# The wide stage of a fused attention and expert kernel: a chunk's small products in one visit of TensorE

## The chip, the cores and the metric

One core of one Trainium2 chip runs the kernel. The metric is device time in microseconds (us); several runs give a median. The profile is one execution, and its engines are called PE (TensorE), PEld (TensorE's weight load), DVE (VectorE), ACT (ScalarE), POOL (GpSimd) and SP (SyncE).

## The reference, cut to what matters

Three layers run in a row over 4 x 768 tokens: a linear attention with a decaying state for each of 8 heads, a gated layer of width 1536, and a top-1 mixture of 8 experts.

```
for t in range(S):                       # attention, S = 768, D = 48
    cur = einsum('bhd,bhe->bhde', u * k_t, v_t)
    y_t = einsum('bhd,bhde->bhe', r_t, state + cur)
    state = w * state + einsum('bhd,bhe->bhde', k_t, v_t)
gate = sigmoid(x @ w_gate); val = x @ w_val
x = (gate * val) @ w_out
idx = argmax(normed(x) @ normed(emb).T / tau)
out[idx == e] = gate_w * (relu(x[idx == e] @ w1[e]) @ w2[e])
```

## The kernel before

The tokens go in 24 chunks of 128, six to a batch. The attention of a chunk is a chunked form: decay tables are multiplied into r and k, a product of k and r gives the chunk's scores, products of k and v (the **state products**) give what the chunk adds to the state, and y is made of a part from the state and a part from the masked scores. A chunk has two halves of 64 tokens. All these are small f32 products of 64x64 (48 wide for the states), and each lies in one quarter of PE's 128x128 array: its operands lie in one half of the partitions (the **row half**), its result in one half of the output's partitions (the column half). An f32 product of this kind leaves two MATMUL records in the trace, so 8 products read x16.

The functions around the change are these. `at_p` issues POOL's table products (lines 542 to 555). `at_P` makes the state products of a chunk (line 617), 16 of them, or 8 in the last chunk of a batch, where the second half's state isn't needed. `at_Y1` makes 8 products of the masked scores with v (line 637) for the two off-diagonal halves of y, and `at_Y2` makes up to 16 products with the states (line 637, read as `py<-ld,T`) and 8 more with the scores (line 637, `py<-Am,ld`). `native_A` makes the 16 score products of the next chunk (line 594). `at_T` adds the state products to the running state on DVE (lines 628 to 633). `at_X` splits y into two parts for the next layer (lines 686 to 692).

The gated layer is the large work. In the **wide stage** it takes 512 tokens at a time, in 12 steps of 128 features: nine `pgate` products of 128x512 (line 721), ACT's sigmoid (line 730), nine `pval` products, DVE's product (line 734), ACT's and DVE's split into two parts (lines 736 and 738), and then the output products `o` of the step before (line 766). A counter called tick goes up by one after `pgate` and once more after `pval`. A table made ahead sets at which tick a stage of which chunk is emitted: six ticks, three steps, to a chunk. Stage 4 (state products, Y1, then `at_T`) falls between `pgate` and `pval`, stage 5 (Y2, the next chunk's scores) between `pval` and `o`. The words "P visit" and "Y visit" stand below for these two. DVE's dot products for the routing (line 783) are spread over the ticks and stand behind whatever a tick has emitted before.

PSUM has these tiles: two buffers in turn for `pgate` and `pval` (pool `ps_gv`, tag `gv`), four for `o`, and one each of `a0` and `a1`, in which y takes columns 0 to 255 and the state products, then the scores, take columns 256 on. A new tile in a buffer waits until the readers of the old one are done. The constant EARLY is 9; stages of chunks 9 to 23 run in the wide stage.

Of the kernel before, what the change touches and what calls it, by code (L numbers as in the profile page):

```python
# [8 lines left out]
F32 = mybir.dt.float32  # L9
# [7 lines left out]
ALU = mybir.AluOpType  # L17
# [18 lines left out]
EARLY = 9  # L36
# [26 lines left out]
def kernel(  # L63
# [14 lines left out]
    nc = tc.nc  # L78
    P = 128
    NCH = att.shape[0]  # L80
    NT, DM = out.shape
    CPB = 6
# [33 lines left out]
    def follow(ins, before):  # L116

        tc.add_manual_dep(
            ins, before.name,
            mybir.DependencyInfo(mybir.DependencyClass.NoSync, mybir.DependencyReason.DATA), reason="order",  # L120
        )
# [181 lines left out]
    if True:  # L303
# [7 lines left out]
        halves = [slice(HALF * i, HALF * i + HALF) for i in range(2)]  # L311
# [32 lines left out]
        ps_gv = ph1.enter_context(tc.tile_pool(name="ps_gv", bufs=2, space=bass.MemoryType.PSUM))  # L344
        ps_o = ph1.enter_context(tc.tile_pool(name="ps_o", bufs=1, space=bass.MemoryType.PSUM))
        ps_a = ph1.enter_context(tc.tile_pool(name="ps_a", bufs=1, space=bass.MemoryType.PSUM))
# [8 lines left out]
        ld = {}  # L355
# [107 lines left out]
        for i in range(7):  # L463
            n = 1 << i
# [3 lines left out]
        tabKt = c1.tile([P, 8, 48], F32, name="tabKt")  # L468
# [54 lines left out]
        yps = {}  # L523
        pms = {}

        def fields(t):
            rT = t[:, 0:512].rearrange("p (a n) -> p a n", a=4)
            kT = t[:, 512:1024].rearrange("p (a n) -> p a n", a=4)
            kt = t[:, 1024:1408].rearrange("p (h d) -> p h d", h=8)
            v = t[:, 1408:1920].rearrange("p (h d) -> p h d", h=8)  # L530
            r = t[:, 1920:2304].rearrange("p (h d) -> p h d", h=8)
            return rT, kT, kt, v, r
# [9 lines left out]
        def at_products(c):  # L542
            rT, kT, kt, v, r = fields(ld[c])
            if c < EARLY:

                nc.gpsimd.tensor_tensor(r, r, kt, op=ALU.mult)
                nc.gpsimd.tensor_tensor(r, r, ubt, op=ALU.mult)
                rk = ld[c][:, 0:1024].rearrange("p (b a n) -> p b a n", b=2, a=4)
                nc.vector.tensor_tensor(rk, rk, tabs, op=ALU.mult)
            else:  # L550
                nc.gpsimd.tensor_tensor(rT, rT, tabR, op=ALU.mult)
                nc.gpsimd.tensor_tensor(kT, kT, tabK, op=ALU.mult)
                nc.gpsimd.tensor_tensor(r, r, kt, op=ALU.mult)
                nc.gpsimd.tensor_tensor(r, r, ubt, op=ALU.mult)
            nc.gpsimd.tensor_tensor(kt, kt, tabKt, op=ALU.mult)

        def at_s1(c):
            at_sd(c)
            at_diag(c)
# [23 lines left out]
        def native_A(c):  # L583

            rT, kT, kt, v, r = fields(ld[c])
            if c > PERM:
                pas = [t[:, 256:512] for t in yps[c - 1]]
            else:
                pool, tag = (ps_o, f"o{1 if c else 0}") if c < PERM else (ps_a, "a")
                pas = [pool.tile([P, 512], F32, tag=f"{tag}{h}", name=f"pa{h}") for h in range(2)]  # L590
            for p in range(4):
                for h in range(2):
                    for i in halves:
                        nc.tensor.matmul(  # L594
                            pas[h][i, p * HALF:p * HALF + HALF], kT[halves[h], p, i], rT[halves[h], p, i],
                            start=True, stop=True,
                        )
            return pas

        def native_mask(c, pas):  # L600
            Am = ams[c]
            for h in range(2):
# [3 lines left out]
                    pas[h][:, 0:4 * HALF].rearrange("p (a n) -> p a n", a=4),  # L606
                )

        def at_P(c):

            rT, kT, kt, v, r = fields(ld[c])
            yps[c] = [ps_a.tile([P, 512], F32, tag=f"a{h}", name=f"py{h}") for h in range(2)]
            pm = [yps[c][1 - i][:, 256:448].rearrange("p (a d) -> p a d", a=4) for i in range(2)]
            for p in range(4):
                for i in range(1 if c % CPB == CPB - 1 else 2):
                    for h in range(2):
                        nc.tensor.matmul(  # L617
                            pm[i][halves[h], p, :], ld[c][halves[i], 1024 + 48 * (2 * p + h):1088 + 48 * (2 * p + h)],
                            v[halves[i], 2 * p + h, 0:48], start=True, stop=True,
                        )  # L620
            pms[c] = pm

        def at_T(c):

            pm = pms.pop(c)
            t0, t1, t2 = (t[:, :, 0:48] for t in (states[c % 2], states[2], states[(c + 1) % 2]))
            if c % CPB == 0:
                nc.vector.tensor_copy(t1, pm[0])
            else:
                nc.vector.tensor_tensor(t1, t0, pm[0], op=ALU.add)  # L630
            if c % CPB < CPB - 1:
                nc.vector.tensor_tensor(t2, t1, pm[1], op=ALU.add)
                nc.vector.tensor_tensor(t2, t2, pw[:, 7, :].unsqueeze(2).to_broadcast([P, 4, 48]), op=ALU.mult)

        def y_part(c, p, h, i, w, x, begins, last):
            o = yps[c][h][halves[h ^ (p % 2)], p // 2 * P + HALF * i:p // 2 * P + HALF * i + HALF]
            q = nc.tensor.matmul(o, w, x, start=begins, stop=last, skip_group_check=True)  # L637
            return getattr(q, "ins", q)

        def chunk_part(c, p, h, i, begins, last):  # L640
            rT, kT, kt, v, r = fields(ld[c])
            n = 2 * p + h
            y_part(c, p, h, i, v[halves[i], n, :], ams[c][halves[i], n, :], begins, last)

        def at_Y1(c):
            for p in range(4):
                for h in range(2):
                    chunk_part(c, p, h, 1 - h, c % CPB == CPB - 1 and h == 0 and p < 2, not (c % CPB or h == 0))

        def at_Y2(c):  # L650
            rT, kT, kt, v, r = fields(ld[c])
            lead = None
            for i in range(2):
                if c % CPB or i:
                    for p in range(4):
                        for h in (1, 0):
                            d = slice(HALF * h, HALF * h + 48)
                            q = y_part(
                                c, p, h, i, (states[2] if i else states[c % 2])[d, p, :], rT[d, p, halves[i]],
                                False, i != h,  # L660
                            )
                            lead = lead or q
                            if h == 0:
                                follow(q, lead)
            for p in range(4):
                for h in (1, 0):
                    chunk_part(c, p, h, h, False, c >= PERM or (h == 1 and p >= 2))
            if c < PERM:
                py = yps[c]
                y3 = early[:, 3 + c % 2, :]  # L670
                nc.scalar.activation(y3, py[1][:, P:2 * P], AF.Copy)
                for k in range(3):
                    nc.tensor.matmul(
                        py[k // 2][:, k % 2 * P:k % 2 * P + P], early[:, k, :], y3,
                        start=False, stop=True, skip_group_check=True,
                    )
# [33 lines left out]
        open_y = []  # L710
        scores = {}
# [310 lines left out]
        def AFTER(c):  # L1022
            return 3 if c < EARLY else 2
# [41 lines left out]
        begins = {}  # L1065
# [16 lines left out]
        def at_stage(c, st):  # L1082
            if st == -2:
                at_p(c)
            elif st == 1:
                at_s1(c)
            elif st == 2:
                native_mask(c, scores.pop(c) if c in scores else native_A(c))
                open_y.clear()
            elif st == 4:  # L1090
                at_P(c)
                at_Y1(c)
                at_T(c)
                open_y.append(c)
            elif st == 5:
                at_Y2(c)
                if c < NCH - 1:
                    scores[c + 1] = native_A(c + 1)
                else:
                    open_y.clear()  # L1100
            elif st == 6:
                at_X(c)
                if c % 2 == 1:
                    at_D(c)
                if c == 7:
                    list(warm_up(WARM_WIDE))
                if c != EARLY - 1 and c + AFTER(c) < NCH:
                    load_chunk(c + AFTER(c))
# [37 lines left out]
        while threads:  # L1146
            th = min((t for t in threads if met(t[3])), key=lambda t: t[0])
            now, t0, dt, need, name, gen = th
# [67 lines left out]
        for f in range(XF):  # L1216
# [16 lines left out]
            elif f == 5:  # L1233
                q = nc.vector.tensor_scalar(lim[:, 0, :], wd, W_MIN, None, op0=ALU.is_ge)
# [28 lines left out]
        for c in CAPS:  # L1263
            n = 3 if c <= 3 * P else 4
# [152 lines left out]
        for f in range(XF):  # L1417
# [4 lines left out]
            if f == 1:  # L1422
                q = nc.sync.dma_start(out=x0, in_=xs[FIRST:CAP])
# [166 lines left out]
```

## Time and profile before

| | |
|---|---|
| time, median of 3 runs | 813.88 us (813.58 to 814.77) |
| the profiled execution's own time | 814.92 us |
| its span, first to last instruction | 813.0 us |
| PE busy | 794.2 us, 98% of the span |
| PEld busy | 703.7 us, 87% |
| DVE busy | 508.8 us, 63% |
| ACT busy | 318.2 us, 39% |
| POOL busy | 226.8 us, 28% |

The profiled execution took 814.92 us, of which 1.9 us lie outside its span. A busy PE is one with a record in flight; since records of matmuls overlap, what PE work costs is read from the distance between starts, not from the length of a record.

### The profile page before, as it was taken

What the parts mean: (1) busy time and instruction counts of PE and PEld (TensorE: products, weight loads), DVE (VectorE), ACT (ScalarE), POOL (GpSimd) and SP (SyncE); (2) the same over time, 40 slices, a digit from 0 to 9 for tenths busy, and PEclk for the clock granted to TensorE, in tenths of its full rate; (3) what the DMA queues carried; (4) which work ended last, traced back from release to release, by engine and by line L of the source; (5) the groups of instructions that cost most, each with busy time, mean ns of one, the idle gap of its engine ahead of it and who ended that gap; (6) DMA issues with size and microseconds to landing.
All of it is one profiled execution on the core that took longest, in us unless ns stands there. A gap on an engine that the chain in (4) does not pass through costs nothing.

```text
span 813.0 us, 17075 instructions
## 1 busy us (share of the span) xinstructions
PE 794.2 (98%) x6864; PEld 703.7 (87%) x6864; DVE 508.8 (63%) x1248; ACT 318.2 (39%) x659; POOL 226.8 (28%) x257
## 2 busy tenths in 40 slices
PE   7899999999999999999999999999999999999997
PEld 6789998888888888888888888889889989899996
DVE  6999965666556665577576548745585555556640
ACT  5788643221231213212322224234374454566541
POOL 5622137244251515244443210200320210201202
PEclk8699999999999999999999999999999999999999
DMA  8749733122222122030402002270556556465401
GB/s 330 285 175 366 265 129 140 60 70 79 69 79 70 60 75 94 14 115 26 143 2 70 21 31 79 98 239 20 167 153 238 167 193 222 146 204 173 145 1 56
DMA packets 36575, 103.02 MB, mean 127 GB/s; under 512 B 4406, under 2 KB 19462, under 8 KB 33417
## 3 DMA queue, kind: packets, MB, share of 16 engines
q1 hardware_dynamic: 32871, 91.92, 33.1%
q0 software_dynamic: 3616, 9.93, 3.3%
q8 instruction: 56, 0.92, 0.5%
q14 instruction: 30, 0.25, 0.1%
q10 hardware_dynamic: 2, 0.00, 0.0%
HBM read 84.09 MB, written 16.28 MB: 123 GB/s over the span
## 4 chain that ended last, share of the span: by engine, by line
PE 77%; issue 12%; DVE 5%; ACT 3%; POOL 2%; DMA 1%; POOLq 0%; SPq 0%; ACTq 0%; DVEq 0%
PE o L766 18%; PE pval L721 16%; PE pgate L721 16%; PE ph L971 7%; PE y L1344 7%; PE py L637 3%; PE pgv L721 3%; PE py L617 2%; POOL out_dram L1377 2%; DVE x L430 1%; PE py L594 1%; PE y L1358 1%; PE warm L376 1%; DVE x L429 1%; DMA ldr<-in_att_dram 1%
## 5 line engine op out<-in xcount | busy, mean ns | idle before, releaser
L721 PE MATMUL pval<-xt,gv 128*128 128x512 f32 x540 | 137.6, 399 | 0.0
L721 PE MATMUL pgate<-xt,gv 128*128 128x512 f32 x540 | 136.3, 397 | 0.0
L766 PE MATMUL o<-wo,gth 128*128 128x384 f32 x480 | 125.9, 343 | 0.0
L721 PEld LDWEIGHTS pval<-xt,gv 128*128 128x128 f32 x540 | 100.4, 188 | 24.4
L721 PEld LDWEIGHTS pgate<-xt,gv 128*128 128x128 f32 x540 | 100.7, 188 | 19.3
L971 PE MATMUL ph<-xk,we 128*128 128x384 f32 (+6 forms) x576 | 116.7, 349 | 0.0
L783 DVE SCALAR_TENSOR_TENSOR prod<-xr,embb 128x384 f32<-128x384 f32 x168 | 104.6, 623 | 4.2 <-DMA embb<-embd 1.1
L971 PEld LDWEIGHTS ph<-xk,we 128*128 128x128 f32 x576 | 101.9, 188 | 5.9 <-issue 1.2
L1344 PE MATMUL y<-we,ht 128*128 128x384 f32 (+1 forms) x528 | 101.4, 339 | 0.0
L736 ACT ACTIVATE gth<-sgw 128x512 fp32r<-128x512 f32 x60 | 37.9, 631 | 146.0 <-DVE sgw L734 146.0
L1344 PEld LDWEIGHTS y<-we,ht 128*128 128x128 f32 (+1 forms) x528 | 91.7, 187 | 1.0
L766 PEld LDWEIGHTS o<-wo,gth 128*128 128x128 f32 x480 | 86.1, 188 | 4.2
L730 ACT ACTIVATE sgw<-pgate 128x512 f32<-128x512 f32 x60 | 35.8, 597 | 126.5 <-PE pgate L721 121.6
L734 DVE TENSOR_TENSOR sgw<-pval,sgw 128x512 f32<-128x512 f32 x60 | 41.4, 690 | 65.6 <-PE pval L721 54.0
L766 PE MATMUL o<-wo,gtl 128*128 128x384 f32 x240 | 81.1, 338 | 0.0
L575 POOL TENSOR_TENSOR Am<-near,sd 128x512 f32<-128x512 f32 (+4 forms) x24 | 27.2, 1132 | 165.1 <-DVE sd L563 122.1
L1377 POOL DMA_INDIRECT out_dram<-yo,xrow x26 | 26.6, 1022 | 166.5 <-ACT yo L1374 154.4
L885 DVE TENSOR_TENSOR we<-wraw,we 128x768 fp32r<-128x768 f32 x64 | 61.7, 967 | 13.6 <-ACT we L882 12.7
L976 DVE SCALAR_TENSOR_TENSOR ht<-ph,ht 128x384 fp32r<-128x384 f32 (+1 forms) x56 | 31.8, 568 | 61.2 <-ACT ht L975 61.0
L738 DVE TENSOR_TENSOR gtl<-sgw,gth 128x512 fp32r<-128x512 f32 x60 | 45.2, 754 | 29.5 <-ACT gth L736 29.4
L975 ACT ACTIVATE ht<-ph 128x384 fp32r<-128x384 f32 (+1 forms) x56 | 28.1, 503 | 81.8 <-PE ph L971 80.4
L721 PE MATMUL pgv<-xt,gv 128*128 128x256 f32 x432 | 58.2, 288 | 0.4 <-DVE gv L438 0.2
(251 smaller groups left out, 1130.5 us busy)
## 6 DMA issues: line engine op xcount, KB each, us to landing
wraw<-in_wex_dram SPq DMA_DIRECT2D x64, 384.0 KB, 3.3
ld<-in_att_dram SPq DMA_DIRECT2D x20, 1152.0 KB, 5.8
raw<-in_wgv_dram SPq DMA_DIRECT2D x12, 768.0 KB, 8.1
w2f<-in_wex_dram SPq DMA_DIRECT2D x10, 768.0 KB, 6.6
xs<-zt SPq DMA_DIRECT2D x8, 750.0 KB, 7.4
raw<-in_wout_dram SPq DMA_DIRECT2D x6, 768.0 KB, 11.4
xrow<-xs SPq DMA_DIRECT2D x6, 600.0 KB, 5.2
ldr<-in_att_dram SPq DMA_DIRECT2D x3, 1152.0 KB, 6.4
```

What stands on the lines that cost most here:

```text
L721: nc.tensor.matmul(pg, a, x[:, k, b, :], start=(n == 0), stop=(n == 8))
L730: nc.scalar.activation(sg, p0, AF.Sigmoid)
L734: nc.vector.tensor_tensor(sg, p1, sg, op=ALU.mult)
L736: nc.scalar.activation(hi, sg, AF.Copy)
L738: q = nc.vector.tensor_tensor(lo, sg, hi, op=ALU.subtract)
L766: nc.tensor.matmul(po[g][t], gt[a][:, ts_], w[:, f % 2, b, :], start=(f == 0 and n == 0), stop=(f == NF - 1 and n == 2))
L783: nc.vector.scalar_tensor_tensor(prod, xr[:, t, 0:DM], 1.0, embb[0][:, e], op0=ALU.mult, op1=ALU.mult, accum_out=xr[:, t, 384 + e:385 + e],)
L885: nc.vector.tensor_tensor(w[:, 768:1536], r, w[:, 0:768], op=ALU.subtract)
L971: nc.tensor.matmul(ph, a, x[:, k, b, :], start=(n == 0), stop=(n == 8))
L976: nc.vector.scalar_tensor_tensor(ht[:, 1, :], ph, 0.0, ht[:, 0, :], op0=ALU.max, op1=ALU.subtract)
L1344: nc.tensor.matmul(yo[e, t], ht[:, a, :], b, start=(f == 0 and n == 0), stop=(f == XF - 1 and n == 2))
L1377: q = nc.gpsimd.indirect_dma_start(out=out, out_offset=bass.IndirectOffsetOnAxis(ap=xrow[e][t].bitcast(I32)[:, 393:394], axis=0), in_=o, i ...
```

## The change

From chunk 10 on the P visit is gone. Everything small of a chunk c is done in one visit at stage 5, between `pval` and `o`: Y1 of chunk c, the state products of chunk c + 1 whose operands lie in the first row half, an instruction that lets TensorE run empty (a drain), Y2 of chunk c, the state products of chunk c + 1 of the second row half, and the scores of chunk c + 1. `at_T` of chunk c + 1 follows on DVE. The state products get PSUM tiles of their own out of the two `gv` buffers, where they lay beside y before. Chunk 9 keeps its P visit, and its Y visit takes the state products of chunk 10. [...] On POOL the product of k with its table moves ahead of r's last one.

```diff
@@ at_products
                 nc.gpsimd.tensor_tensor(r, r, kt, op=ALU.mult)
+                nc.gpsimd.tensor_tensor(kt, kt, tabKt, op=ALU.mult)
                 nc.gpsimd.tensor_tensor(r, r, ubt, op=ALU.mult)
+                return
             nc.gpsimd.tensor_tensor(kt, kt, tabKt, op=ALU.mult)
@@ new functions
+        def state_part(c, p, i):
+            rT, kT, kt, v, r = fields(ld[c])
+            for h in range(2):
+                nc.tensor.matmul(
+                    pms[c][i][halves[h], p, :], ld[c][halves[i], 1024 + 48 * (2 * p + h):1088 + 48 * (2 * p + h)],
+                    v[halves[i], 2 * p + h, 0:48], start=True, stop=True,
+                )
+        def whole_visit(c):
+            n = c + 1
+            states_of = [lambda: None]
+            if n < NCH:
+                pms[n] = [
+                    ps_gv.tile([P, 512], F32, tag="gv", name="pm")[:, 0:192].rearrange("p (a d) -> p a d", a=4)
+                    for i in range(1 if n % CPB == CPB - 1 else 2)
+                ]
+                states_of = [lambda i=i: [state_part(n, p, i) for p in range(4)] for i in range(len(pms[n]))]
+            if c > EARLY:
+                open_tiles(c)
+                open_y.append(c)
+                waits = []
+                def wait():
+                    d = nc.tensor.drain()
+                    waits.append(getattr(d, "ins", d))
+                parts = [lambda: at_Y1(c), states_of[0], wait, lambda: at_Y2(c)] + states_of[1:]
+            else:
+                parts = [lambda: at_Y2(c)] + states_of
+            if n < NCH:
+                parts.append(lambda: scores.update({n: native_A(n)}))
+            in_turn(*parts)
+            if n < NCH:
+                at_T(n)
+            else:
+                open_y.clear()
@@ at_Y1
-                    chunk_part(c, p, h, 1 - h, c % CPB == CPB - 1 and h == 0 and p < 2, not (c % CPB or h == 0))
+                    begins = p < 2 and (c > EARLY or (c % CPB == CPB - 1 and h == 0))
+                    chunk_part(c, p, h, 1 - h, begins, not (c % CPB or h == 0))
@@ at_stage
-            elif st == 4:
+            elif st == 4 and c <= EARLY:
                 at_P(c)
                 at_Y1(c)
                 at_T(c)
                 open_y.append(c)
+            elif st == 5 and c >= EARLY:
+                whole_visit(c)
             elif st == 5:
                 at_Y2(c)
-                if c < NCH - 1:
-                    scores[c + 1] = native_A(c + 1)
-                else:
-                    open_y.clear()
+                scores[c + 1] = native_A(c + 1)
```

`in_turn` only keeps the parts in this order on PE, and `at_P` of the chunks up to 9 calls `state_part` in the old order.

On PE, the P visit of chunk 12 before: line 617 is the state products (`py` with the higher number is the tile of the first row half, the other that of the second), line 637 is Y1.

```order
L721 MATMUL pgate<-xt,gv 128x512 x9
L617 MATMUL py_2845<-ld 64x48 x2
L617 MATMUL py_2844<-ld 64x48 x2
L617 MATMUL py_2845<-ld 64x48 x2
L617 MATMUL py_2844<-ld 64x48 x2
L617 MATMUL py_2845<-ld 64x48 x2
L617 MATMUL py_2844<-ld 64x48 x2
L617 MATMUL py_2845<-ld 64x48 x2
L617 MATMUL py_2844<-ld 64x48 x2
L637 MATMUL py_2844<-Am,ld 64x64
L637 MATMUL py_2845<-Am,ld 64x64
```

On PE, after, the middle of chunk 11's visit, in which the first eight state products of chunk 12 stand (`pm`, line 625); the drain stands between `pm` and the first row with `T_200`, and is not among the printed rows.

```order
L684 MATMUL py_2651<-Am,ld 64x64
L684 MATMUL py_2650<-Am,ld 64x64
L684 MATMUL py_2651<-Am,ld 64x64
L625 MATMUL pm<-ld 64x48 x8
L684 MATMUL py_2651<-ld,T_200 64x64
L684 MATMUL py_2650<-ld,T_200 64x64
L684 MATMUL py_2651<-ld,T_200 64x64
```

And, after, the end of the same visit on PE: Y2's last products, the other eight state products, the scores (line 596).

```order
L684 MATMUL py_2651<-Am,ld 64x64
L684 MATMUL py_2650<-Am,ld 64x64
L625 MATMUL pm<-ld 64x48 x8
L596 MATMUL py_2650<-ld 64x64 x2
L596 MATMUL py_2651<-ld 64x64 x2
L596 MATMUL py_2650<-ld 64x64 x2
L596 MATMUL py_2651<-ld 64x64 x2
```

Where the state products went from one row half to the other by turns, they now stand as eight of one half in a row, twice.

On DVE, chunk 13 before: the state's three operations (lines 630 to 633) and two dots stand ahead of `pval`'s product (the second line 734).

```order
L734 TENSOR_TENSOR sgw<-pval,sgw 128x512
L738 TENSOR_TENSOR gtl<-sgw,gth 128x512
L630 TENSOR_TENSOR T_201<-T_200,py_3066 128x4x48
L632 TENSOR_TENSOR T_199<-T_201,py_3065 128x4x48
L633 TENSOR_TENSOR T_199<-T_199,pn 128x4x48
L783 SCALAR_TENSOR_TENSOR prod,xr<-xr,embb 128x384 x2
L734 TENSOR_TENSOR sgw<-pval,sgw 128x512
L738 TENSOR_TENSOR gtl<-sgw,gth 128x512
```

On DVE after, at the same step (lines 782 and 786 are 734 and 738 of before, 677 to 680 the state, now of chunk 14):

```order
L782 TENSOR_TENSOR sgw<-pval,sgw 128x512
L786 TENSOR_TENSOR gtl<-sgw,gth 128x512
L831 SCALAR_TENSOR_TENSOR prod,xr<-xr,embb 128x384 x2
L782 TENSOR_TENSOR sgw<-pval,sgw 128x512
L786 TENSOR_TENSOR gtl<-sgw,gth 128x512
L677 TENSOR_TENSOR T_201<-T_199,pm 128x4x48
L679 TENSOR_TENSOR T_200<-T_201,pm 128x4x48
L680 TENSOR_TENSOR T_200<-T_200,pn 128x4x48
```

The state's operations moved behind the step's product and split, and read `pm`, one of the two `gv` buffers.

## Rows read from the trace of the kernel before

**Rows 1.** Stages: stretch, length, busy PE, PEld, DVE, ACT, POOL, clock, DMA share, GB/s.

```profile
160.00:545.30 385.30, 385.30 (x3481) 328.46 (x3481) 240.87 (x667) 98.44 (x211) 122.65 (x133) 1.00 0.21 73
545.30:813.00 267.70, 261.53 (x1501) 241.38 (x1499) 140.35 (x333) 128.86 (x257) 40.05 (x50) 0.99 0.45 146
```

**Rows 2.** PE's timeline (start, length, line), chunk 13: a plain step, then one with visits.

```profile
237.80 2.28 PE L721 MATMUL pgate<-xt,gv 128*128 128x512 f32 x9
239.91 2.27 PE L721 MATMUL pval<-xt,gv 128*128 128x512 f32 x9
242.01 0.51 PE L766 MATMUL o<-wo,gth 128*128 128x384 f32 x2
...
244.13 2.25 PE L721 MATMUL pgate<-xt,gv 128*128 128x512 f32 x9
246.32 0.68 PE L617 MATMUL py<-ld 64*64 64x48 f32 x32
246.82 0.43 PE L637 MATMUL py<-Am,ld 64*64 64x64 f32 x16
247.18 2.37 PE L721 MATMUL pval<-xt,gv 128*128 128x512 f32 x9
249.48 0.69 PE L637 MATMUL py<-ld,T 48*64 48x64 f32 x32
...
250.23 0.65 PE L594 MATMUL py<-ld 64*64 64x64 f32 x32
250.80 0.62 PE L766 MATMUL o<-wo,gth 128*128 128x384 f32 x2
...
253.03 0.39 PE L721 MATMUL pgate<-xt,gv 128*128 128x512 f32 x1
```

**Rows 3.** PE's timeline, P visit of chunk 11, whose state products lie in one row half.

```profile
203.29 0.49 PE L617 MATMUL py<-ld 64*64 64x48 f32 x10
203.58 0.27 PE L637 MATMUL py<-Am,ld 64*64 64x64 f32 x1
...
203.80 0.41 PE L637 MATMUL py<-Am,ld 64*64 64x64 f32 x12
204.14 0.50 PE L721 MATMUL pval<-xt,gv 128*128 128x512 f32 x1
```

**Rows 4.** Lengths by line: operation, count, minimum/median/maximum in ns; then PE's restart after DVE.

```profile
L617 PE MATMUL py<-ld x624: 218/218/340, 15.4 to 463.0; 64*64 64x48 f32 x156
...
L1585 PEldq DRAIN  x2: 8/8/8, 808.6 to 812.5; - x2
...
40.43 1.19 DVE L992 TENSOR_TENSOR ld<-ld,tabs 128x1024 f32<-128x1024 f32 x1
...
41.73 0.69 PE L594 MATMUL pa<-ld 64*64 64x64 f32 x32 [0.76 <-PE py L637]
```

**Rows 5.** PE's timeline, steps of chunk 12 and of chunk 23, the last.

```profile
222.82 2.25 PE L721 MATMUL pgate<-xt,gv 128*128 128x512 f32 x9
...
231.48 0.39 PE L721 MATMUL pgate<-xt,gv 128*128 128x512 f32 x1
...
460.33 2.27 PE L721 MATMUL pgate<-xt,gv 128*128 128x512 f32 x9
465.67 0.69 PE L637 MATMUL py<-ld,T 48*64 48x64 f32 x32
...
466.53 0.62 PE L766 MATMUL o<-wo,gth 128*128 128x384 f32 x2
...
468.75 0.64 PE L721 MATMUL pgate<-xt,gv 128*128 128x512 f32 x2
```

**Rows 6.** DVE, chunk 13's Y visit; POOL, chunk 19's last; PE, chunk 18's Y visit.

```profile
249.66 0.69 DVE L734 TENSOR_TENSOR sgw<-pval,sgw 128x512 f32<-128x512 f32 x1
...
355.42 1.01 POOL L555 TENSOR_TENSOR ld<-ld,tabKt 128x384 f32<-128x384 f32 x1
...
357.57 0.46 PE L637 MATMUL py<-ld,T 48*64 48x64 f32 x16
```

More of the change, by code (lines that the diff above doesn't have):

```diff
@@ L607, in native_mask, with open_tiles @@
                 )
+        def open_tiles(c):
+            yps[c] = [ps_a.tile([P, 512], F32, tag=f"a{h}", name=f"py{h}") for h in range(2)]
         def at_P(c):
-            rT, kT, kt, v, r = fields(ld[c])
-            yps[c] = [ps_a.tile([P, 512], F32, tag=f"a{h}", name=f"py{h}") for h in range(2)]
-            pm = [yps[c][1 - i][:, 256:448].rearrange("p (a d) -> p a d", a=4) for i in range(2)]
+            open_tiles(c)
+            pms[c] = [yps[c][1 - i][:, 256:448].rearrange("p (a d) -> p a d", a=4) for i in range(2)]
@@ L614, in at_P @@
             for p in range(4):
                 for i in range(1 if c % CPB == CPB - 1 else 2):
[L616 to L621, printed above, removed]
+                    state_part(c, p, i)
+        def state_part(c, p, i):
[5 more added lines that the diff above has]
+                )
@@ new lines, in in_turn @@
+        def in_turn(*parts):
+            last = None
+            for part in parts:
+                first = len(nc.cur_bb.bb.instructions)
+                part()
+                new = [q for q in nc.cur_bb.bb.instructions[first:] if q.engine == mybir.EngineType.PE]
+                if last is not None and new:
+                    follow(new[0], last)
+                last = (new or [last])[-1]
+        def whole_visit(c):
[8 more added lines that the diff above has]
+            if c > EARLY:
+                open_tiles(c)
+                open_y.append(c)
[13 more added lines that the diff above has]
+                open_y.clear()
```

## The prediction

> **What bounds the kernel now.** I read the stages first. From 160 to 545 us PE has a record in flight all the time, at a granted clock of 1.00, and from there to the end for 261.53 of 267.70 us, while DVE is busy for 241 of the first 385 us [rows 1]. So a microsecond put into or taken out of PE's row in the wide stage should reach the end nearly whole, and other engines matter only where PE would have to wait for them. Then I read PE's timeline, by the distance between starts. A plain step is 2.11 us of `pgate`, 2.10 of `pval`, 2.12 of `o`, together 6.33. The step of chunk 13 with both visits is 253.03 - 244.13 = 8.90, so the two visits cost 2.57 us [rows 2]: 0.08 on the way in (2.19 in place of 2.11), 0.86 for state products and Y1, 0.20 around `pval` (2.30 in place of 2.10), 0.75 for Y2, and 0.68 for the scores and the way out (250.23 to 253.03, less 2.12). A chunk comes by every 21.5 us or so; counted from chunk 9, the P visits at 203.29 and 246.32 are those of chunks 11 and 13.
>
> The third thing to see is the pace of small products. In chunk 13 the 32 records of state products start within 0.50 us, 15 ns apart, going from one row half to the other by turns [rows 2]. In chunk 11, the last of its batch, only the eight products of the first row half exist, and the first ten of their records start within 0.49 - 0.22 = 0.27 us, 30 ns apart [rows 3]. Half the work took the same time: that P visit lasts 0.85 us (203.29 to 204.14) against 0.86. So each row half has a pace of its own, 30 ns a record, and 15 ns comes about only when both halves have work.
>
> **What goes.** From chunk 10 to 23 the P visit leaves its place: 14 ways in, ways out and slow starts of `pval`. They are in the 2.57 us, and none is costed apart.
>
> **What comes, for an ordinary chunk.** The visit starts with Y1 and eight state products of the first row half. That is exactly the content of chunk 11's P visit, in another order, and there the last record starts at 203.80 + 0.41 - 0.22 = 203.99 and gives way 0.03 later: 0.73 us [rows 3]. Then the drain, D. Then Y2, 0.75 as before. Then the other eight state products, 16 records in the second row half: 16 x 0.030 = 0.48. The scores that follow need both halves, so the second half has this on top of a load that was even, and I take all of it as added. Scores and way out stay 0.68, the way in 0.08. Sum 0.08 + 0.73 + 0.75 + 0.48 + 0.68 = 2.72 + D, against 2.57: **0.15 + D slower.**
>
> **D, the drain.** No row shows one inside PE's work. The only rows of one take 8 ns, on an engine with nothing left to do [rows 4]; this is the lower end, 0.01 us. A nearer row below: between chunk 11's last small product and the full-array `pval` lie 0.15 us (203.99 to 204.14), 0.12 over the usual 0.03; there the array has to finish too before it is used in another shape [rows 3]. From above: a small product runs 218 ns from its start [rows 4], and after a wait PE starts again 0.11 us after the operation that it waited for (DVE's line 992 ends at 40.43 + 1.19 = 41.62, PE starts at 41.73; the row names an older product of PE, long done) [rows 4]. Last product to its end, then a restart, less the gap that is there anyway: 0.22 + 0.11 - 0.03 = **0.30, which I take**, since the drain is a wait that must see the end and then let the sequencer go on. If the end is seen later than the record shows, by another 0.22, it is 0.52. No gain is possible from it.
>
> [...]
>
> **The other chunks.** Chunks 12 and 18 begin a batch: their steps cost 231.48 - 222.82 - 6.33 = 2.33 [rows 5] because Y2 has half the state part, 0.24 less, and the visit after has it less too: again 0.15 + D. Chunks 10, 16 and 22 are followed by the last chunk of a batch, which has no second eight: 2.72 - 0.48 = 2.24 + D against 2.57, that is D - 0.33. Chunk 23 has none to prepare: before, 468.75 - 460.33 - 6.33 = 2.09; after, 0.08 for the way in, Y1 alone with 16 x 0.015 = 0.24, D, Y2 with way out 0.86 (465.67 to 466.53), 0.10 at `o` [rows 5]: 1.28 + D, that is D - 0.81. Chunk 9 keeps both visits and gets chunk 10's products, eight of one half, then eight of the other: 0.96 in a row, 0.48 if side by side. In chunk 11 the first Y1 record of the other half started 0.29 us after the first state product, 0.19 before these were through [rows 3], so 0.96 - 0.19, some 0.76.
>
> Sum: 10 chunks x 0.15 = 1.50; 3 x -0.33 = -0.99; -0.81; +0.76. Together **0.46 + 14 D**, with D = 0.30 **4.7 us**.
>
> **What hides the rest.** The first eight write the buffer of `pgate`, whose sigmoid is done two microseconds before. The second eight write that of `pval`, and wait for DVE's product: it ends at 250.35, 0.87 us after the Y visit's start at 249.48 [rows 2, 6], and is needed 0.73 + 0.30 + 0.75 = 1.78 after it: 0.9 to spare. DVE also has `at_T` no longer ahead of it. The next `pgate` waits until DVE has read the first `pm`. That read follows the product, ACT's copy and DVE's split, a chain of three operations of some 0.7 us, so it ends about 2.6 us into a visit that, with `o` behind it, lasts 5; behind it on PE would stand the whole next step. POOL's product of k with its table must now be done before the visit: chunk 19's ended at 356.43, chunk 18's Y visit began at 357.57 [rows 6], and the move ahead of r's last product brings it forward by one operation of about 1 us. The row sum that waits for r on DVE comes that much later, and DVE takes it a visit later. No transfer and no queue of SP's changes place. None of this costs anything by these rows.
>
> **Rivals.** *Faster.* The pace of 30 ns could be no property of the row half, and eight products of one half cost 0.24 us as they would by turns. Then an ordinary chunk is 0.08 + 0.48 + 0.75 + 0.24 + 0.68 = 2.23 + D, -0.34 + D; the three -0.58 + D, chunk 23 as above, chunk 9 +0.48: -5.5 + 14 D. With D = 0.30 that is -1.3 us, 812.6; with 0.12 it is -3.8, 810.1; it is faster by more than 0.2% for D under 0.27. For it speaks only that rows 3 are chunks of a special kind; chunk 11 speaks against it.
>
> [...]
>
> *The drain is cheap.* If PE is empty sooner than the records say, D = 0.12 gives +2.1 us, 816.0; D = 0.01, a drain that does not hold PE at all, gives +0.6, 814.5, no difference that can be told. For it: 0.12 is the one row of the array changing over. Against it: the sequencer has no part in that row.
>
> *A new wait for a buffer.* If DVE is late with `pval`'s product, ten visits wait in their middle. One more operation of 0.69 in front of it stays hidden by 0.2; two would cost 0.47 each time, 4.7 us on top of the forecast, 823.2. Against it: the only dots ahead of it fitted before, with `at_T` besides.
>
> **How the numbers follow.** The three runs' median is 813.88 us; the profiled execution took 814.92, 1.0 more, so its counterpart should show about 819.6. The forecast is 813.88 + 4.7 = 818.5 us. Chances: forecast with D from 0.15 to 0.55 (816.4 to 822.0) 0.68; cheap drain 0.12, of it 0.05 under a gain or loss of 0.2%; even pace 0.13, half of it faster and half within 0.2%; new wait 0.07. A measurement of this kernel tells about 0.2%, 1.6 us, from no change. So faster 0.07, same 0.12, slower 0.81. The range runs from the cheapest drain to D = 0.55: 814.5 to 822.1; outside lie the even pace and the new wait.
>
> **What would show it.** Right: in the trace after, an ordinary step with a visit lasts some 9.3 us (6.33 + 2.72 + 0.30) where it lasted 8.90, a hole of about 0.3 us between the first `pm` and Y2, and 0.48 us from the second `pm` to the scores. Wrong: a hole under 0.15 or over 0.5; `pm` records 15 ns apart; PE waiting at the second `pm` or the next `pgate` for DVE; a granted clock under 1.00 in the stage.

## The result, and the profile after

| | before | after |
|---|---|---|
| time, median | 813.73 us (813.36 to 814.77, 4 runs) | 818.57 us (817.98 to 819.07, 4 runs) |
| the profiled execution's own time | 814.92 us | 818.71 us |
| its span | 813.0 us | 816.9 us |
| first to last `pgate` of the wide stage | 411.83 us | 416.93 us |
| step with visits, chunk 11 | 8.89 us | 9.33 us |

The changed kernel is slower by 4.8 us: ratio 1.0057, 95% interval 1.0040 to 1.0075. The forecast was 818.5 us.

First the whole of the stage, by the view of stretches (stretch, length, busy PE, PEld, DVE, ACT, POOL, clock, DMA share, GB/s) of the changed kernel. It answers to the first of [rows 1].

```profile
160.00:545.30 385.30, 383.44 (x3413) 330.17 (x3413) 244.93 (x665) 98.23 (x208) 123.30 (x133) 1.00 0.21 70
```

The clock is still 1.00, and PE, which before had a record in flight all the time, is now without one for 385.30 - 383.44 = 1.86 us. That is less than half of what was lost: most of the loss looks like busy time, because records of small products overlap (one of the first `pm` is 218 ns long, and 29 ns lie from start to start) and the view counts a half-used array as busy. So the loss has to be read from distances between starts. PE's timeline of the changed kernel (start, length, line), chunk 11's plain step and the step with its visit, answers to [rows 2] and, for the new drain, to nothing there:

```profile
194.36 2.26 PE L769 MATMUL pgate<-xt,gv 128*128 128x512 f32 x9
196.45 2.26 PE L769 MATMUL pval<-xt,gv 128*128 128x512 f32 x9
198.56 0.52 PE L814 MATMUL o<-wo,gth 128*128 128x384 f32 x2
...
200.67 2.28 PE L769 MATMUL pgate<-xt,gv 128*128 128x512 f32 x9
202.79 2.27 PE L769 MATMUL pval<-xt,gv 128*128 128x512 f32 x9
...
204.98 0.46 PE L684 MATMUL py<-Am,ld 64*64 64x64 f32 x16
205.27 0.63 PE L625 MATMUL pm<-ld 64*64 64x48 f32 x16
206.00 0.69 PE L684 MATMUL py<-ld,T 48*64 48x64 f32 x32
206.51 0.42 PE L684 MATMUL py<-Am,ld 64*64 64x64 f32 x16
206.74 0.46 PE L625 MATMUL pm<-ld 64*64 64x48 f32 x10
206.99 0.28 PE L596 MATMUL py<-ld 64*64 64x64 f32 x2
207.02 0.29 PE L625 MATMUL pm<-ld 64*64 64x48 f32 x4
...
207.16 0.70 PE L596 MATMUL py<-ld 64*64 64x64 f32 x28
207.78 0.62 PE L814 MATMUL o<-wo,gth 128*128 128x384 f32 x2
...
210.00 2.26 PE L769 MATMUL pgate<-xt,gv 128*128 128x512 f32 x9
```

The plain step is 6.31 us, as good as the 6.33 of before. The step with the visit is 210.00 - 200.67 = 9.33 us, so beyond 6.33 the visit costs 3.00 where two visits cost 2.57. Its pieces by starts: 0.08 on the way in (204.98 - 202.79 = 2.19 in place of 2.11); Y1 and the first `pm`, 16 records each, whose last starts at 205.27 + 0.63 - 0.22 = 205.68, so 0.73 with the 0.03 to the next start; a hole of 206.00 - 205.71 = 0.29 for the drain; 0.74 for Y2 (206.00 to 206.74); 1.04 for the second `pm` and the scores, where the scores alone took 0.57 before; 0.10 in the first `o`. The sixteen records of the first `pm` begin in pairs, one for each column half, 0.63 - 0.22 = 0.41 us from the first to the last; once they run, a pair follows a pair after 0.058 us, so 29 ns a record.

The other chunks' steps, by the same distance from `pgate` to `pgate`: chunk 9 went from 8.89 to 9.65, chunks 10, 16 and 22 became 0.03 shorter (chunk 10 from 8.90 to 8.87), 12 and 18 from 8.66 to 9.10, chunk 23 from 8.42 to 7.96, the remaining eight from 8.89 to 9.33. Summed, 0.76 - 0.09 + 0.88 - 0.46 + 3.52 = 4.6 us. Of the 5.1 us by which the stage as a whole grew in this trace, 0.65 belong to a single wait in a step without a visit (looked at below). Ahead of the stage the profiled execution was 1.1 us shorter than that of before (first `pgate` at 139.81 in place of 140.93), which is why its own time is 3.8 and not 4.8 us longer.

### The profile page after: what moved, and what is told of

Same layout as the page of the kernel before. It is cut to its first block, busy times and chain, and to the rows that moved or that the text cites. A ratio compares the mean times of both kernels' runs of the same rounds, so it can differ in the third digit from the quotient of the medians.

```text
span 816.9 us, 17099 instructions
## 1 busy us (share of the span) xinstructions
PE 796.7 (98%) x6864; PEld 709.1 (87%) x6864; DVE 515.1 (63%) x1248; ACT 319.4 (39%) x659; POOL 226.3 (28%) x257
## 4 chain that ended last, share of the span: by engine, by line
PE 56%; issue 5%; ACT 2%; POOL 1%; DMA 1%; DVE 1%; POOLq 0%; ACTq 0%; DVEq 0%
PE o L814 11%; PE pgate L769 10%; PE pval L769 10%; PE ph L1019 10%; PE y L1391 9%; PE py L684 1%; PE y L1405 1%; PE pt L1356 1%; POOL out_dram L1424 1%; PE pm L625 1%; PE ph L1483 1%; DMA wraw<-in_wex_dram 1%; PE py L596 1%; ACT L139 0%; ACT we L930 0%
## 5 line engine op out<-in xcount | busy, mean ns | idle before, releaser
L831 DVE SCALAR_TENSOR_TENSOR prod<-xr,embb 128x384 f32<-128x384 f32 x168 | 109.4, 651 | 3.3 <-ACT xr L824 0.3
```

The source lines that it names most:

```text
L831: nc.vector.scalar_tensor_tensor(prod, xr[:, t, 0:DM], 1.0, embb[0][:, e], op0=ALU.mult, op1=ALU.mult, accum_out=xr[:, t, 384 + e:385 + e],)
```

## The experiments

The theory going in: the loss is two things, the drain (0.29 us in each of 14 visits) and the order of the state products, eight of one row half in a row, which runs at the pace of one half (29 ns a record in the trace after). The first rival says that the order is free and the drain is all; the second that a state product has the pace of 29 ns in its new tile, whatever the order.

### The state products by turns

All 16 state products behind Y2, from one row half to the other by turns; the drain stays, between Y1 and Y2.

```diff
-                states_of = [lambda i=i: [state_part(n, p, i) for p in range(4)] for i in range(len(pms[n]))]
+                states_of = [lambda: [state_part(n, p, i) for p in range(4) for i in range(len(pms[n]))]]
-                parts = [lambda: at_Y1(c), states_of[0], wait, lambda: at_Y2(c)] + states_of[1:]
+                parts = [lambda: at_Y1(c), wait, lambda: at_Y2(c)] + states_of
```

> The changed kernel, but all 16 state products of the next chunk stand behind Y2 and go from one row half to the other by turns, as they did before the change; the first eight are no longer ahead of the drain. Theory (row half and drain): 32 records by turns cost 0.50 us as in the P visit of before. An ordinary visit is then 0.08 in, 0.29 Y1, 0.27 drain, 0.75 Y2, 0.50 state products, 0.68 scores and way out, together 2.57 us, the same as both visits of before: steps of 8.90 us where the changed kernel has 9.33. Chunk 9 gains 0.50 in place of 0.76, chunk 23 loses 0.46 as it does now: 813.7 us in all, no change against the kernel before. Rival one (29 ns a record is what a state product costs into its new tile, whatever the order): 32 records cost 0.94, steps stay at 9.3 and the time at 818.6 us. Rival two (the whole loss is the drain's, the order is free): 818.6 us too, with 15 ns a record in the trace and a hole of over 0.6 us in front of Y2.

Measured: 814.79 us (11 runs) against 814.15 of the kernel before (15 runs), ratio 1.0003, 95% interval 0.9994 to 1.0012. Steps of 8.89 us. PE's timeline of this kernel, chunk 11's visit:

```profile
205.89 0.46 PE L684 MATMUL py<-Am,ld 64*64 64x64 f32 x16
206.47 0.69 PE L684 MATMUL py<-ld,T 48*64 48x64 f32 x32
206.98 0.42 PE L684 MATMUL py<-Am,ld 64*64 64x64 f32 x16
207.21 0.64 PE L625 MATMUL pm<-ld 64*64 64x48 f32 x32
207.66 0.67 PE L596 MATMUL py<-ld 64*64 64x64 f32 x32
208.26 0.62 PE L814 MATMUL o<-wo,gth 128*128 128x384 f32 x2
```

The 32 `pm` records take 207.66 - 207.21 = 0.45 us, 14 ns each, into the same new tiles. The drain's hole is still there: Y1's last record starts at 205.89 + 0.46 - 0.22 = 206.13 and Y2 at 206.47, 0.34, against 0.04 between such groups elsewhere: 0.30. So both rivals fall, and 0.44 us of an ordinary visit's loss is the order of eight and eight. Two steps of this trace miss the forecast. Chunk 9's is 9.59, 0.70 more than before where 0.50 was expected: Y1 and the drain do not stand ahead there, so the products of the second half, whose tile is `pval`'s buffer, are reached before DVE has read it (its product ends at 163.86, the first of them starts at 163.91). Chunk 21's is 9.05, since its drain lasted 647 ns where the others lasted some 492; why is not known.

### The halves in the kernel before

The order alone, without drain, tiles or moves: the P visit of before with eight products of one half, then eight of the other.

```diff
-            for p in range(4):
-                for i in range(1 if c % CPB == CPB - 1 else 2):
+            n = 1 if c % CPB == CPB - 1 else 2
...
+            for p, i in [(p, i) for i in range(n) for p in range(4)] if c > EARLY else [(p, i) for p in range(4) for i in range(n)]:
```

> The kernel before with the state products of its P visit in another order from chunk 10 on: eight of the first row half, then eight of the second, in place of turns. No drain, no other tile, nothing moved (11 chunks have both halves). Theory: 16 records of one half at 30 ns, 0.96 for both, of which 0.19 overlap, as in chunk 9 of the changed kernel: 0.77 in place of 0.50, 0.27 more in each of 11 steps: 816.7 us. Rival (even pace, the order is free): 813.7 us, no change, and 15 ns a record in the trace.

Measured: 817.54 us against 814.15, ratio 1.0041, 95% interval 1.0027 to 1.0055, so 2.2 to 4.5 us where 3.0 were expected. The steps of the eleven chunks grew by 0.26 to 0.29 us each, 3.1 in all; those of chunks 11, 17 and 23, with one half, not at all. PE's timeline, chunk 13's P visit of this kernel, against the second step of [rows 2]:

```profile
247.09 0.89 PE L619 MATMUL py<-ld 64*64 64x48 f32 x29
...
248.22 2.37 PE L727 MATMUL pval<-xt,gv 128*128 128x512 f32 x9
```

From the first state product to `pval` it is 248.22 - 247.09 = 1.13 us where it was 0.86. Here the second eight begin while the first still run (29 records start within 0.89 - 0.22 = 0.67 us, where 29 ns from each to the next would make 0.81), so the price is 0.27; in the changed kernel Y2 stands between the two eights. The first eight have nothing to run beside, and the second only the scores, half of which need the second row half too: the two groups together took 1.04 us where the scores alone took 0.57. There the price is 0.44.

### The drain alone

The kernel before with a drain between Y2 and the scores of chunks 10 to 23, all else as it was.

```diff
                 at_Y2(c)
+                if c > EARLY:
...
+                    d = nc.tensor.drain()
...
                 if c < NCH - 1:
                     scores[c + 1] = native_A(c + 1)
```

> The kernel before with one thing added: in chunks 10 to 23 TensorE runs empty between Y2 and the next chunk's scores (14 drains, nothing else moved). Theory: each costs what the trace of the changed kernel shows in front of Y2, 0.25 to 0.28 us; in chunk 23 nothing small follows and the way to o is paid anyway, some 0.1. Together 3.4 to 3.8 us: 817.1 to 817.5 us. Rival (the drain is cheap, 0.12, and the hole in front of Y2 has another cause, such as the first product of a bank): 815.4 us. Rival (the whole loss of the changed kernel is the drain's, some 0.74 an ordinary chunk): 824 us.

Measured: 821.02 us against 814.15, ratio 1.0084, 95% interval 1.0070 to 1.0098: 6.9 us, nearly twice the theory and short of the rival. PE's timeline, chunk 13's Y visit, then the scores' line in a window of 0.15 us there (operation, count, minimum/median/maximum in ns, first and last start), and last, from the trace of before, the group of Y2 that [rows 2] leaves out:

```profile
249.94 0.69 PE L637 MATMUL py<-ld,T 48*64 48x64 f32 x32
250.45 0.41 PE L637 MATMUL py<-Am,ld 64*64 64x64 f32 x16
251.12 0.69 PE L594 MATMUL py<-ld 64*64 64x64 f32 x32 [0.25 <-issue]
251.74 0.62 PE L766 MATMUL o<-wo,gth 128*128 128x384 f32 x2
```

```profile
L594 PEldq EVENT_SEMAPHORE  x1: 51/51/51, 251.0 to 251.0; - x1
L594 PEld LDWEIGHTS py<-ld x1: 129/129/129, 251.1 to 251.1; 64*64 64x64 f32 x1
```

```profile
249.99 0.41 PE L637 MATMUL py<-Am,ld 64*64 64x64 f32 x16
```

From Y2's last group to the scores it is 0.67 us where before it was 0.24 (249.99 to 250.23), and the scores take 0.62 where they took 0.57: 0.48 a chunk, seen in every step of chunks 10 to 22 (9.37 for 8.89 in most); in chunk 23, where `o` follows, it is 0.23. Another 0.3 of this trace lies in one plain step where the rank products wait. PE stands without any record for 0.25 us, twice the 0.12 in front of Y2 in the run with turns (205.89 + 0.46 = 206.35 to 206.47). Part of what lies in it is the first row of the second view: the first score has two waits, one of which is an instruction of its own on PE's sequencer, 51 ns long. In the trace of before the same instruction stands ahead of its time, at 250.0, while Y2's products are still running and the scores start at 250.23:

```profile
L594 PEldq EVENT_SEMAPHORE  x1: 51/51/51, 250.0 to 250.0; - x1
```

So here what the sequencer used to do ahead of time stands open behind the drain. The records' own times give the size: from the drain's end to the next product it is 0.17 us, against 0.06 in the changed kernel. The drain also ends 0.08 us after the last product's record, against 0.04 there, and no run shows why. The next run moves the wait instruction.

### The drain one product later

The drains of chunks 10 to 22 once more, 13 of them, behind the first score product, which carries the waits, and not ahead of it.

```diff
+                        if c > EARLY + 1 and (p, h, i) == (0, 0, halves[0]):
...
+                            d = nc.tensor.drain()
```

> The kernel before with a drain in chunks 10 to 22 (13 drains), as in the run with drains ahead of the scores, but one product later: the first score product, which carries the scores' two waits, stands ahead of the drain, the other fifteen behind it. There each drain cost 0.48 us, and the trace shows a wait instruction of 0.05 us between the drain's end and the first score, which before had been dealt with 0.25 us ahead of its product. Theory (what a drain costs is the last product's end, some 0.05 to 0.08 until the drain is over, the start of the next, and every wait instruction that stands behind it): without the wait instruction 0.29 to 0.34 each, 3.8 to 4.4 us in 13: 817.8 to 818.4 us against 814.0 of the kernel before. Rival (a drain in this place costs 0.48 whatever stands behind it, since work of another kind follows): 6.2 us, 820.2 us.

Measured: 820.25 us against 814.25, ratio 1.0072, 95% interval 1.0059 to 1.0086; the steps with visits grew by some 0.41 us each. As a total this lies at the rival and well outside the theory; the timeline says why. Two windows of it around the drain of chunk 13, PE's records of the first score product and the weights of the next:

```profile
251.81 0.28 PE L595 MATMUL py<-ld 64*64 64x64 f32 x2
```

```profile
252.16 0.15 PEld L595 LDWEIGHTS py<-ld 64*64 64x64 f32 x4 [0.21 <-issue]
```

The lone first product leaves two records, the second at 251.81 + 0.28 - 0.22 = 251.87, 58 ns after the first: both lie in the same quarter of the array, and in the first `pm` of the changed kernel too a quarter's next record came after 0.058 us. The next weights are loaded at 252.16, and their product starts right behind: 0.30 us from start to start, as in front of Y2 in the changed kernel (205.68 to 206.00 is 0.32), where the drain ahead of the scores had 251.12 - 250.64 = 0.48. So with the wait instruction out from behind the drain the hole is some 0.17 shorter. That work of another kind follows can't be what made it dear: in the changed kernel Y2 follows state products, at 0.32. But here the lone product costs 0.06, and the fifteen products behind the drain take 0.62 (up to `o` at 252.79) where all sixteen took 0.57: 0.06 + 0.30 + 0.62 = 0.98 for 0.57, the 0.41. The total was mis-sized, since the run moved one cost and added others. It is the rows, and not the time, that tell the two apart.

### Two drains in a row

```diff
                     d = nc.tensor.drain()
...
+                    e = nc.tensor.drain()
```

> The changed kernel with a second drain right behind each of its 14. Theory (the price is the running out and the restart, which the second finds done): the second adds its 8 ns, as on an idle engine, and the 0.05 to 0.07 us from one instruction to the next that the trace shows behind a drain: 14 x 0.06 to 0.08, 0.8 to 1.1 us, 819.2 to 819.8 us. Rival (a drain has a price of its own of 0.3 us wherever it stands): 4.2 us, 822.7 us.

Measured: 822.14 us (820.80 to 823.09) against 814.25, ratio 1.0096, 95% interval 1.0081 to 1.0112. The drains' own lines in this kernel, the first and the second of each pair:

```profile
L656 PEldq DRAIN  x14: 492/747/748, 185.3 to 472.7; - x14
L659 PEldq DRAIN  x14: 13/13/13, 186.1 to 473.3; - x14
```

The first lasts 747 ns mostly, since it starts while the products ahead of it still run; the second lasts 13 ns. The steps with visits grew from 9.33 to 9.41, that is 0.08 a pair, 1.1 us in all, as the theory has it: the second finds PE empty. The time grew by more, and by itself it would speak for the rival's 822.7. In the trace, 1.6 us beyond the steps with visits lie in the two plain steps behind chunk 16's visit (6.60 and 7.65 us); most of it is one wait of PE for DVE:

```profile
PE pval L772 <- DVE sgw L785: 1.1, 1, 1.1
```

```profile
DVE xt L743 <- ACT xt L742: 6.6, 1, 6.6
...
ACT xr L827 <- DMA xs<-xr,pi: 3.5, 1, 3.5
```

(who waited for whom, us in total, times, longest; the first for PE, the others in the same stretch.) A scatter of the routing landed late and held up ACT, behind it DVE (POOL waited 5.4 us for it; in the stage of the changed kernel its longest such wait was 1.9). Whether the second drains brought that about, or an execution's chance, is open: against the kernel before, this one is 7.9 us slower and the changed kernel 4.8, and 1.1 of the 3.0 between them is accounted for in every step.

### The changed kernel once more

> The changed kernel once more, unaltered, for its trace. In the first trace one step without a visit (the third after chunk 14's visit) lasted 7.16 us in place of 6.51, since TensorE waited there for the mask, the mask for GpSimd and GpSimd for a load that took 6.9 us from issue to use where the trace of before has 5.1. Theory one (chance of that execution's transfers): 6.51 us here. Theory two (the change brings it about): 7.1 to 7.2 us again at the same step. Time 817.5 to 819 us in both.

Measured: 819.09 us, one run. In the first trace of the changed kernel the rank products waited in the second plain step behind chunk 14's visit (the third, if the visit's own is counted). PE's waits in the stage and its timeline there:

```profile
PE pr L883 <- DVE Am L605: 0.5, 1, 0.5
```

```profile
282.20 2.28 PE L769 MATMUL pgate<-xt,gv 128*128 128x512 f32 x9
...
287.06 0.18 PE L883 MATMUL pr<-cum,ones 128*128 128x16 bf16 x1 [0.48 <-DVE Am L605]
...
289.36 0.85 PE L769 MATMUL pgate<-xt,gv 128*128 128x512 f32 x3
```

In the second trace PE waits for nothing in the stage, and that step is 289.94 - 283.45 = 6.49 us:

```profile
283.45 2.26 PE L769 MATMUL pgate<-xt,gv 128*128 128x512 f32 x9
...
289.94 2.28 PE L769 MATMUL pgate<-xt,gv 128*128 128x512 f32 x9
```

Every other step of the stage agrees with the first trace to 0.03 us, and from the first `pgate` to the last it is 416.28, 4.45 more than before. So the wait of 0.65 us is not a fixed part of the change. GpSimd's first operation on the load, in the first trace and in the second:

```profile
279.91 1.29 POOL L552 TENSOR_TENSOR ld<-ld,tabs 128x512 f32<-128x512 f32 x1 [10.22 <-DMA ld<-in_att_dram]
```

```profile
280.23 1.30 POOL L552 TENSOR_TENSOR ld<-ld,tabs 128x512 f32<-128x512 f32 x1 [9.03 <-DMA ld<-in_att_dram]
```

It starts 2.3 us ahead of the step's first `pgate` in the first trace and 3.2 in the second, the load having taken 6.9 and 6.0 us. But the change may have a share in how often the wait occurs. In the five traces of kernels with one visit this operation starts 2.3 to 3.4 us ahead of that step, in the four with two visits 3.6 to 4.2. The wait at this step came again in one of the runs below, and in no trace of a kernel with two visits.

### An order without the drain

If order and drain are the whole loss, an order that needs neither should win. Y2 first, then the scores, the state products by turns, and Y1 last. In the changed kernel the drain keeps Y1 and the other row half's products in its bank apart in time (Y2 starts 0.10 us behind the end of the last record ahead of it). Here a read of one score column by ACT, for which Y1 waits, does that while the state products run.

```diff
-                states_of = [lambda i=i: [state_part(n, p, i) for p in range(4)] for i in range(len(pms[n]))]
+                states_of = [lambda: [state_part(n, p, i) for p in range(4) for i in range(2)]]
...
+                parts = [lambda: at_Y2(c)]
...
+                    def scores_first():
...
+                        scores[n] = native_A(n)
...
+                        q = nc.scalar.activation(hop, scores[n][1][:, 4 * HALF - 1:4 * HALF], AF.Copy)
...
+                    parts += [scores_first] + states_of
...
+                parts.append(y1_last)
```

> The changed kernel in a third order: Y2, the next chunk's scores, its state products by turns (both halves, also in the last chunk of a batch), and Y1 last. No drain: what keeps Y1 apart from the products of the other row half in its bank is a read of one column by ScalarE, which waits for the last score and which Y1 waits for, while the state products run. The start flags of a bank move from Y1 to Y2. Chunk 23 keeps a drain. Theory: 0.08 in, 0.75 Y2, 0.50 scores, 0.50 state products, 0.29 Y1, 0.15 out: 2.27 us against 2.57, steps of 8.6 us, if the wait is hidden. The read can start when ScalarE's split of the step is done, some 1.55 us into the visit, and the state products give out at 1.83, so PE should wait 0 to 0.15. In all 13 chunks x -0.30 to -0.15, chunk 9 +0.50, chunk 23 -0.46: 809.8 to 811.8 us, faster than the kernel before. Rival (the read comes late, behind ScalarE's other work, and PE runs empty for half a microsecond each time): 816 us or more, and the trace shows Y1 waiting for ScalarE.

Measured: 811.28 us (5 runs) against 814.15, ratio 0.9961, 95% interval 0.9947 to 0.9974: faster than both kernels. Steps of 8.61 us where before has 8.89. PE's timeline, chunk 11's visit, ACT's in the same stretch, and the only one of the waits for the read that the view of waits lists, in chunk 18's visit:

```profile
206.06 0.69 PE L718 MATMUL py<-ld,T 48*64 48x64 f32 x32
206.58 0.41 PE L718 MATMUL py<-Am,ld 64*64 64x64 f32 x16
206.81 0.65 PE L597 MATMUL py<-ld 64*64 64x64 f32 x32
207.28 0.63 PE L626 MATMUL pm<-ld 64*64 64x48 f32 x32
207.75 0.46 PE L718 MATMUL py<-Am,ld 64*64 64x64 f32 x16
208.15 0.62 PE L848 MATMUL o<-wo,gth 128*128 128x384 f32 x2
```

```profile
206.96 0.63 ACT L818 ACTIVATE gth<-sgw 128x512 fp32r<-128x512 f32 x1 [2.30 <-DVE sgw L816]
207.53 0.17 ACT L668 ACTIVATE hop<-py 128x1 f32<-128x1 f32 x1
```

```profile
PEld py L718 <- ACT hop L668: 0.2, 1, 0.2
```

The read ends at 207.70 and Y1 starts at 207.75. It starts 0.05 us behind the read in twelve of the thirteen visits, so it is the read that lets Y1 go. That is just late: from the last state product's start to Y1's it is 0.06 us in chunk 11 and most others, 0.02 more than from group to group elsewhere. Where the state products end earlier against the read, PE stands longer: the same distance is 0.10 in chunk 12, 0.14 in chunk 16 and 0.24 in chunk 18. So the expected wait of 0 to 0.15 holds but for chunk 18. Five groups follow each other at the pace of turns (the scores and the state products 32 records in 0.47 us each, 15 ns a record). The step is 0.28 us shorter than in the run with turns and a drain, about the drain's price once more. In its profiled execution, 812.79 us, the rank products' wait of 0.5 us came again, at the same step.

## Why the prediction was right, point by point

**The sum.** An ordinary chunk was put at 0.15 + D slower, 0.45; measured 0.44. Chunks 10, 16 and 22 at D - 0.33, -0.03; measured -0.03. Chunk 23 at D - 0.81, -0.51; measured -0.46. Chunk 9 at +0.76; measured 0.76. Together 4.7 against 4.6 by the steps and 4.8 by the times. Only the guess at the profiled execution was off: it was put at 819.6, since the one of before lay 1.0 above its median, and took 818.71. That surplus did not carry over.

**The pace of a row half.** Taken from [rows 3] as 30 ns a record against 15 by turns, it held in the new place: 29 ns in the `pm` groups, and 14 by turns in the same tiles. The even pace, the one rival that would have made the change a gain, is refuted by the run with turns and by the halves in the kernel before.

**The drain.** Taken as 0.30, the last product's 0.22 to its end and 0.11 for a restart, less the gap of 0.03; measured 0.29 in chunk 11 and 0.30 with turns. The restart is there too: from the end of the last product's record to Y2 it is 0.10. The drain does see that end: its own record ends 0.04 us later, and Y2 starts 0.06 behind it. The cheap drain, 0.12 or 0.01, is out. The row behind the 0.12 does not show an array that had to finish first: `pval` starts there at 204.14, 0.07 us ahead of the end of the last small product's record (203.99 + 0.22 = 204.21). The size, though, was right for this place alone: ahead of the scores of the kernel before, the hole is 0.48, and a wait instruction behind the drain explains the larger part of the difference (0.17 us from the drain's end to the next product in place of 0.06; 0.30 for the whole hole with that instruction ahead of the drain).

**What hides the rest.** The buffers held. DVE and PE of the changed kernel, in one visit (from 270.86):

```profile
271.04 0.69 DVE L782 TENSOR_TENSOR sgw<-pval,sgw 128x512 f32<-128x512 f32 x1 [0.30 <-PE pval L769]
...
273.49 0.35 DVE L679 TENSOR_TENSOR T<-T,pm 128x192 f32<-128x192 f32 x1
```

```profile
272.62 0.46 PE L625 MATMUL pm<-ld 64*64 64x48 f32 x10
...
275.88 0.39 PE L769 MATMUL pgate<-xt,gv 128*128 128x512 f32 x1
```

`pval`'s product is done at 271.73 and its buffer is written again at 272.62, 0.9 to spare, as put; DVE's last read of a `pm` ends at 273.84, 2.0 before `pgate` is due. PE waited for neither in the stage, so the rival of a new buffer wait is out too for the changed kernel; by turns it did come, once, in chunk 9.

**What was not seen.** The rank products' wait for the mask. The prediction looked at POOL's product of k and at the tiles, and not at how near the mask comes to its deadline when a load lands late. In the trace of before PE did not wait for it. It was worth 0.65 us in one trace of two.

**Signs that were read too simply.** "A hole of about 0.3 us between the first `pm` and Y2" is true from the last record's start; from its end only 0.10 us are empty (205.27 + 0.63 = 205.90 to 206.00), and a view of busy time shows the drain as a third of what it costs. And from the second `pm` to the first score it is not 0.48 but 0.25 us (206.74 to 206.99): scores of the other row half start beside the state products. The cost is there all the same, 1.04 - 0.57 = 0.47, since the scores of the second half come later.

## What to carry to other kernels

Small products that each fill a quarter of the array kept their pace in these traces, 14 to 15 ns a record, only while both row halves had work, and with one half at work it was 29 to 30; an order that ran one half and then the other, with other work between, cost as much again as the products took by turns (0.44 on 0.45 us), and 0.27 where the two halves could overlap. Price a drain in a stretch of small products from the last record's start to the next record's start, and look for instructions with waits behind it, since in these traces a wait that had been dealt with in advance stood open there (0.17 us from the drain's end to the next product in place of 0.06). Where two groups must not overlap, a wait on another engine's small read, issued while a third group runs, can do the drain's work for less: here for 0.02 us in most visits and 0.2 in the worst, in place of 0.3.

## What the runs showed of the hardware beyond that

A drain's price depended on what stood behind it: from the last start to the next it was 0.30 to 0.34 us ahead of a plain product and 0.48 ahead of one with a wait instruction of its own (51 ns long). A second drain right behind the first lasted 13 ns and cost 0.08 us. And the scores behind a drain took some 0.05 us longer (32 records in 0.62 us in place of 0.57).
